# Gathers that leave out the rows of small loads, folds in halves with one job per step, and a store job of its own: a Fourier mixing layer followed by a squared-ReLU feed-forward layer

## The chip, the cores and the metric

The kernel runs on one core of one Trainium2 chip. The metric is the device time of one launch in microseconds (us). Three launches of the kernel before took 628.2, 628.49 and 630.97 us; their median, 628.49 us, is the time before. About 0.5% (3 us) is what a measurement of this kernel can tell from no change.

## The reference, cut to what matters

```
x: (8, 3008, 256) float32      w_in: (256, 2048)      w_out: (2048, 256)
X = fft(fft(x, axis=1), axis=2).real          # per batch of 3008 rows
t = X.reshape(24064, 256)
out = maximum(t @ w_in, 0) ** 2 @ w_out       # float32 (24064, 256)
```

Only the real part is wanted, so the transform along the 3008 rows is a pair of cosine and sine sums, and the transform along the 256 columns can be folded into `w_in`. Rows k and S-k of one batch come from the same two sums with a sign turned, so the kernel computes them together, as a "plus" and a "minus" row.

## The kernel before, in words

**Windows and stages.** The 24064 output rows are computed as 25 windows (`w` = 0 to 24) of up to 512 columns k, each giving a plus and a minus row. Windows 6 to 23 are alike, 512 wide. A window w >= 2 runs eight stages s = 0 to 7; a stage makes 256 of the 2048 hidden features. The order of the instructions on every engine is the order in which the Python code issues them (the schedule is manual); engines wait for each other only through semaphores.

**A plain stage** (`pq`, `turn`): TensorE makes four matmuls of cosines and sines into one PSUM tile `ph` (L808, L809), then 16 matmuls of the second layer of the window before (L679), then two matmuls (L831) that turn the tile into the minus rows. ScalarE applies ReLU to the tile before and after the turn (L840), VectorE squares both (L847).

**A differential stage** (those in `diff[w]`, from window 6 on mostly 0, 2, 4, 6) saves two matmuls: TensorE makes the two cosine matmuls alone (L817); VectorE at once forms `t2` = -2 x cosines + n2 (`twice`, L821); after the 16 matmuls of L679 TensorE adds the sines (L826); ScalarE takes the plus rows out of `ph` (L840) and squares them (L851), VectorE makes the minus rows from `t2` and `ph` in one custom operation (L838). The sines overwrite what `twice` reads, so **L826 waits for L821**, and L821 waits for `n2`, which GpSimd computes with two operations per stage (`nyq_rows`, L769) from a tile `zn` (L760, L761). The rows for window w+1 are issued in the last stages of window w.

**Folds.** The spectrum sums of a batch need its rows added and subtracted in pairs first. Batch number i (0 to 7; the batch index is `bs[i]` = 1 to 7, then 0) is loaded by `load_x` into one buffer `xo` of four quarters (128 partitions x 6 rows of 256 values each, float32 turned into float16 on the way), all from GpSimd's DMA queue: quarters 0 and 1 by a plain DMA (L127), quarters 2 and 3, which must come in reversed row order, by indirect gathers over row indices (L132). Three places need a patch. Row 0 of the batch has to stand in the first place of quarter 2, and for the usual batch VectorE copies it there from quarter 0 (L417; L393 in the first fold). The last batch of `bs` order but one (b = 7, i = 6) has no row after its end to gather, so its index list `idx_c` points the first two partitions to a harmless place, and a small load (L150) overwrites partition 1. Batch 0 (i = 7) has no row before its start, so a gather with the index list `idx_f` fetches quarter 0, and a small load (L143) overwrites one row. The small loads write where a gather has written, and so wait for that gather to land.

**Fold jobs.** `fold_steps(i)` gives the steps: `d_even` (L417 to L419: the copy, then 128x3072 sums into `fe`, then a 128x24 copy), `d_odd` (L422, differences into `fo`), `n_cos` (L429), `n_sin` (L432), `odds` (L435), `even` (L447, and straight after it the store of the folded rows to DRAM, L449), `back` (four loads of these rows in another layout, L457 and L459), `nyq` (two tiny matmuls and a VectorE copy, L440 to L442), and four `late` steps (L473 twice, L484 twice, the last of them followed by the four small copies L490 to L492 of `nyq8`). All sums are VectorE's. For i >= 2 the loop at L728 to L742 places these jobs by hand into the stages: with `b0` = 5, 8, 10, 13, 16, 19 for i = 2 to 7, `d_even` and `n_cos` go to stages 1 and 3 of window b0-1 (5 and 7 for i = 2 and 4), `d_odd` to stage 0 of window b0, `n_sin` and `odds` both to stage 1, `even` and `nyq` to stage 3, `back` to 6, the next `load` to 7, and the late steps to stages 3, 3, 5, 7 of window b0+1. Within a stage these jobs (`others`) are issued after `twice` and the squares of the stage before, and ahead of L838. For i = 0 and 1 the jobs are placed in windows 0 to 4 by the loop over windows (L779 to L796).

Of the kernel before, what the change touches and what calls it, by code (L numbers as in the profile page):

```python
# [12 lines left out]
AF = mybir.ActivationFunctionType  # L13
ALU = mybir.AluOpType

HS = 32.0
P = 128
R = 6


def rev_dim(ap, i):

    dims = [list(d) for d in ap.ap]
    step, cnt = dims[i]
    dims[i] = [-step, cnt]
    return bass.AP(tensor=ap.tensor, offset=ap.offset + step * (cnt - 1), ap=dims)
# [3 lines left out]
def kernel(  # L30
# [51 lines left out]
    def win_of(col):  # L82
        return max(w for w in range(NW) if wins[w][0] <= col) if col < TOT else NW
# [5 lines left out]
    col_of = {}  # L89
# [26 lines left out]
    XW = R * D  # L116

    def load_x(i, first=lambda: None):
        b = bs[i]
        t = xp.tile([P, 4, R, D], F16, name="xo", tag="xo")  # L120
        o = b * S * D

        def flat(q):
            return t[:, q, :, :].rearrange("p c d -> p (c d)")

        def direct(q0, q1):
            nc.gpsimd.dma_start(  # L127
                out=t[:, q0:q1, :, :].rearrange("p q c d -> p q (c d)"),
                in_=bass.AP(tensor=x.tensor, offset=x.offset + o + (q0 * H - 5) * D, ap=[[XW, P], [H * D, q1 - q0], [1, XW]]))

        def gather(q, idx, base):
            nc.gpsimd.indirect_dma_start(  # L132
                out=flat(q), out_offset=None,
                in_=bass.AP(tensor=x.tensor, offset=0, ap=[[XW, B * S * D // XW], [1, XW]]),
                in_offset=bass.IndirectOffsetOnAxis(ap=idx, axis=0),
                element_offset=base)

        if b > 0:
            direct(0, 2)
        else:  # L140

            gather(0, idx["f"][:, 0:1], o + D)
            nc.gpsimd.dma_start(out=t[0:1, 0, R - 1, :], in_=bass.AP(tensor=x.tensor, offset=x.offset + o, ap=[[D, 1], [1, D]]))  # L143
            direct(1, 2)
        first()

        gather(2, idx["r" if b + 1 < B else "c"][:, 0:1], o + (S - R * (P - 1)) * D)
        if b + 1 == B:

            nc.gpsimd.dma_start(  # L150
                out=t[1:2, 2, :, :].rearrange("p c d -> p (c d)"),
                in_=bass.AP(tensor=x.tensor, offset=x.offset + o + (S - R) * D, ap=[[XW, 1], [1, XW]]))
        gather(3, idx["r"][:, 0:1], o + (H - R * (P - 1)) * D)
        return t

    def iota(shape, pattern, base, mult, name):
        t = const.tile(shape, I32, name=name)
        nc.gpsimd.iota(t, pattern=pattern, base=base, channel_multiplier=mult)
        return t

    idx = {}
# [28 lines left out]
    idx["c"] = iota([P, 1], [[1, 1]], P - 1, -1, "idx_c")  # L190
    nc.gpsimd.memset(idx["c"][0:2, :], P - 3)
    idx["f"] = iota([P, 1], [[1, 1]], -1, 1, "idx_f")
    nc.gpsimd.memset(idx["f"][0:1, :], 0)
# [114 lines left out]
    at = const.tile([P, 2, P + 1], F32, name="at")  # L308
# [6 lines left out]
    spn = fop.tile([P, 2, 2, P], F16, name="spn")  # L315
# [53 lines left out]
    def fold_steps(i):  # L369
        t = xs.pop(i)  # L370
# [12 lines left out]
        st = {}  # L383
        xf = t.rearrange("p q c d -> p (q c) d")
        lo = xf[:, :, 1:129]
# [27 lines left out]
                nc.vector.tensor_copy(ev[:, :, 0, 0:1], w[:, :, 0:1])  # L413
            nc.gpsimd.memset(ev[:, :, sg, 129:130], 0.0)

        def d_even():
            nc.vector.tensor_copy(t[0:1, 2, 0, :], t[0:1, 0, R - 1, :])  # L417
            nc.vector.tensor_tensor(fef[:, :, 1:129], lo, hi, op=ALU.add)
# [47 lines left out]
        def fold8(sg):  # L466
            if sg == 0:
                xy = fop.tile([P, 12, 260], F16, name="xy", tag="xy")
                xt = st["xt"] = xy[:, 0:8].rearrange("p (g s r) d -> p g s r d", g=2, s=2)
                yt = st["yt"] = xy[:, 8:12].rearrange("p g (s r d) -> p g s r d", s=1, r=2).rearrange("p (g c) s r d -> p g (c s) r d", g=2)  # L470
                folded[i, 1] = (xt, yt)
            rb = st["rb"]
            nc.vector.tensor_tensor(st["xt"][:, sg], rb[:, 0:2], rev_dim(rb[:, 2:4], 2), op=ALU.subtract if sg else ALU.add)  # L473

        def fold16(sg):

            xt, yt = st["xt"], st["yt"]
# [6 lines left out]
            nc.vector.tensor_tensor(yt[:, sg], both(0), rev_dim(both(1), 2), op=ALU.subtract if sg else ALU.add)  # L484

        def nyq8():

            xt, yt = st["xt"], st["yt"]
            for slot in range(2):
                nc.vector.tensor_copy(xt[:, 0, slot, :, 130:131], rev_dim(xt[:, 1, 1 - slot, :, 128:129], 1))  # L490
# [231 lines left out]
    def put(d, w, s, i, name):  # L722
        d[w][s].append(lambda: folds[i][name]())

    def make(i):
        folds[i] = fold_steps(i)

    for i in range(2, B):  # L728
        b0 = (win_of(col_of[i, 0]) + win_of(col_of[i - 1, 1])) // 2 - 1
        both = i > 2 and len(at_of[b0 - 1][3]) > 0  # L730
        at_of[b0 - 1][0 if i > 2 else 5].append(lambda i=i: make(i))
        put(at_of, b0 - 1, 5 if i == 2 or both else 1, i, "d_even")
        put(at_of, b0 - 1, 7 if i == 2 or both else 3, i, "n_cos")
        for s, name in ((0, "d_odd"), (1, "n_sin"), (1, "odds"), (3, "even"), (6, "back"), (7, "load")):
            put(at_of, b0, s, i, name)
        put(post_of, b0, 3, i, "nyq")
        if b0 > 5:
            diff[b0] = (2, 4, 6)
        for st in range(4):
            at_of[b0 + 1][(3, 3, 5, 7)[st]].append(lambda i=i, st=st: folds[i]["late"][st]())  # L740
        if both:
            diff[b0 - 1] = (2, 6)  # L742
# [29 lines left out]
    for w in range(NW):  # L772
# [231 lines left out]
```

## Time and profile before

| what | value |
|---|---|
| median of three launches | 628.49 us (628.2 to 630.97) |
| the profiled execution | 630.0 us, its span 628.0 us, mean granted TensorE clock 0.994 |
| TensorE (PE) busy | 94% |
| VectorE (DVE) busy | 77% |
| ScalarE (ACT) busy | 73% |
| GpSimd (POOL) busy | 54% |
| moved by DMA | 47.50 MB, mean 76 GB/s |

The span runs from the program's first instruction to its last; some 2 us of the launch lie outside. Busy shares are means over all windows. PE is the engine with the least idle time, so a stall is read best as the idle time in brackets ahead of a PE instruction in the timeline, with the engine and line that ended it. The order of the windows in time follows from the first L808 or L817 of each: for example window 7 starts at 163.56 us, 12 at 290.16, 15 at 365.18, 18 at 443.41, 21 at 522.38.

### The profile page before, as it was taken

To read this page: it belongs to the slowest core of one execution; us is meant where nothing else is said; L and a number is where in the kernel's file an instruction comes from. 1 tells how busy PE (TensorE), PEld (TensorE's weight loads), DVE (VectorE), ACT (ScalarE), POOL (GpSimd) and SP (SyncE) were. 2 spreads that over 40 slices of the span, in tenths; PEclk is the share of its full clock that TensorE was granted. 3 is DMA by queue.
4 is the path that set the end of the run, shared out by engine and by line. 5 is a ranking of instruction groups with operands and counts; after the bars stand their busy time and mean duration, and the time that the engine had idled before them with its cause. 6 is when DMAs were issued, how large, how long until landed. Compare 5 with 4: busy or idle time off the path is not lost.

```text
span 628.0 us, 11263 instructions
## 1 busy us (share of the span) xinstructions
PE 592.7 (94%) x4441; PEld 427.6 (68%) x4441; DVE 484.2 (77%) x607; ACT 460.7 (73%) x624; POOL 338.9 (54%) x248
## 2 busy tenths in 40 slices
PE   4889999999999999999899979999799999999997
PEld 2457786676666776776677746777467776777786
DVE  7787666978888679878887868878588788777760
ACT  6687777878777776877687856878468787787762
POOL 8220225268808617498086673865838558538520
PEclk9999999999999999999999989999899999999999
DMA  8945321124511461236113431132511311111112
GB/s 150 141 89 131 111 69 33 46 81 84 119 41 43 111 137 43 73 78 133 45 36 106 101 74 49 38 108 66 104 33 50 103 47 49 47 39 44 52 55 67
DMA packets 36523, 47.50 MB, mean 76 GB/s; under 512 B 4215, under 2 KB 30327, under 8 KB 36471
## 3 DMA queue, kind: packets, MB, share of 16 engines
q0 software_dynamic: 9344, 22.14, 17.7%
q1 hardware_dynamic: 26899, 24.44, 13.1%
q8 instruction: 34, 0.56, 0.4%
q10 hardware_dynamic: 228, 0.21, 0.1%
q14 instruction: 18, 0.15, 0.1%
HBM read 33.63 MB, written 27.84 MB: 98 GB/s over the span
## 4 chain that ended last, share of the span: by engine, by line
PE 65%; DVE 13%; POOL 9%; DMA 6%; issue 4%; ACT 3%; POOLq 0%; DVEq 0%
PE po L679 37%; PE ph L831 5%; PE ph L808 5%; PE ph L809 5%; POOL n L769 5%; PE ph L826 5%; PE ph L817 3%; PE pz L567 3%; DVE t L821 3%; DVE h L847 3%; DVE h L838 3%; ACT h L840 2%; DMA xo<-in_x_dram,idx_c 2%; DMA xo<-in_x_dram,idx_f 2%; DMA xo<-in_x_dram,idx_r 1%
## 5 line engine op out<-in xcount | busy, mean ns | idle before, releaser
L840 ACT ACTIVATE h<-ph 128x1024 f16<-128x1024 f32 (+3 forms) x311 | 295.6, 990 | 102.2 <-PE ph L826 82.7
L679 PE MATMUL po<-wout,h 128*128 128x256 f16 (+1 forms) x3024 | 362.8, 273 | 0.0
L769 POOL TENSOR_SCALAR n<-zn,g2n 128x512 f32<-128x512 f16 (+2 forms) x146 | 264.8, 1829 | 165.8 <-ACT zn L761 165.5
L679 PEld LDWEIGHTS <-h 128*128 128x128 f16 (+1 forms) x3024 | 297.2, 99 | 73.1 <-issue 1.3
L847 DVE TENSOR_TENSOR h<-h 128x1024 f16<-128x1024 f16 (+6 forms) x216 | 193.8, 908 | 33.4 <-ACT h L840 30.7
L838 DVE CUSTOM_DVE_ANT_0 h<-t,ph 128x1024 f16<-128x1024 f32 x67 | 81.8, 1221 | 47.7 <-ACT h L840 47.3
L821 DVE SCALAR_TENSOR_TENSOR t<-ph,n 128x1024 f32<-128x1024 f32 (+2 forms) x73 | 87.6, 1200 | 29.7 <-PE ph L817 22.3
L808 PE MATMUL ph<-zc,gh 128*128 128x512 f16 (+3 forms) x238 | 88.4, 372 | 0.4 <-ACT h L900 0.3
L809 PE MATMUL ph<-zs,gh 128*128 128x512 f16 (+3 forms) x238 | 88.4, 372 | 0.0
L851 ACT ACTIVATE h<-h 128x1024 f16<-128x1024 f16 (+2 forms) x73 | 76.1, 1043 | 0.0
L831 PE MATMUL ph<-zs,gh 128*128 128x512 f16 (+3 forms) x238 | 68.1, 368 | 0.0
L694 ACT ACTIVATE osb<-po 128x512 f32<-128x512 f32 (+3 forms) x95 | 55.2, 585 | 11.4 <-PE po L679 10.0
L826 PE MATMUL ph<-zs,gh 128*128 128x512 f16 (+2 forms) x146 | 43.6, 380 | 17.0 <-DVE t L821 16.9
L817 PE MATMUL ph<-zc,gh 128*128 128x512 f16 (+2 forms) x146 | 42.8, 375 | 0.0
L809 PEld LDWEIGHTS <-gh 128*128 128x128 f16 x238 | 23.4, 98 | 26.4 <-issue 1.9
L808 PEld LDWEIGHTS <-gh 128*128 128x128 f16 x238 | 23.4, 98 | 25.7 <-issue 1.1
L826 PEld LDWEIGHTS <-gh 128*128 128x128 f16 x146 | 13.8, 97 | 22.6 <-issue 19.4
L572 ACT ACTIVATE es<-pz 128x376 f32<-128x376 f32 (+1 forms) x32 | 15.5, 487 | 17.5 <-PE pz L567 17.4
L831 PEld LDWEIGHTS <-gh 128*128 128x128 f16 x238 | 22.1, 98 | 5.4
L817 PEld LDWEIGHTS <-gh 128*128 128x128 f16 x146 | 14.3, 98 | 16.7
L459 POOL DMA_INDIRECT rb<-scr,idx_r x16 | 20.6, 1288 | 4.9 <-issue 4.9
L132 POOL DMA_INDIRECT xo<-in_x_dram,idx_r x15 | 18.3, 1219 | 4.5 <-issue 4.0
(142 smaller groups left out, 355.3 us busy)
## 6 DMA issues: line engine op xcount, KB each, us to landing
out_dram<-osb SPq DMA_DIRECT2D x77, 128.0 KB
xo<-in_x_dram POOLq DMA_DIRECT2D x7, 768.0 KB
scr<-ev POOLq DMA_DIRECT2D x8, 390.0 KB, 2.8
rb<-scr POOLq DMA_DIRECT2D x16, 130.0 KB
out_dram<-osb SPq DMA_DIRECT2D x12, 94.0 KB
w<-in_moe_w_in_dram POOLq DMA_DIRECT2D x2, 512.0 KB, 11.2
wout<-in_moe_w_out_dram POOLq DMA_DIRECT2D x1, 1024.0 KB
out_dram<-osb SPq DMA_DIRECT2D x8, 75.0 KB
```

The source lines that it names most:

```text
L679: nc.tensor.matmul(po[0:m, j * D : (j + 1) * D], h2[:, fc, q : q + m], wout16[:, fc, :], start=(fc == 0), stop=(fc == NFC - 1))
L769: nc.gpsimd.tensor_scalar(out=n2[:, a, 0:wn1], in0=zns[wt][:, 0:wn1], scalar1=g2n[:, fc : fc + 1], scalar2=None, op0=ALU.mult)
L808: nc.tensor.matmul(ph[:, a, 0:wn], gh[:, 0, f0 : f0 + P], zcw[:, 0:wn], start=True, stop=False)
L809: nc.tensor.matmul(ph[:, a, 0:wn], gh[:, 1, f0 : f0 + P], zsw[:, 0:wn], start=False, stop=True)
L817: nc.tensor.matmul(ph[:, a, 0:wn], gh[:, 0, f0 : f0 + P], zcw[:, 0:wn], start=True, stop=True)
L821: nc.vector.scalar_tensor_tensor(out=t2[:, :, 0:wn], in0=phs[s][:, :, 0:wn], scalar=-2.0, in1=n2s[w, s][:, :, 0:wn], op0=ALU.mult, op1=ALU ...
L826: nc.tensor.matmul(phs[s][:, a, 0:wn], gh[:, 1, f0 : f0 + P], zsw[:, 0:wn], start=False, stop=True, skip_group_check=True)
L831: nc.tensor.matmul(phs[s][:, a, 0:wn], gh[:, 2, f0 : f0 + P], zsw[:, 0:wn], start=False, stop=True, skip_group_check=True)
L838: nc.vector._custom_dve(TENSOR_ADD_SAT, out=h, in0=t2s[s][:, :, 0:wn], in1=phs[s][:, :, 0:wn], s0=BIG, s1=0.0)
L840: nc.scalar.activation(h, phs[s][:, :, 0:wn], AF.Relu, bias=0.0, scale=-1.0)
L847: nc.vector.tensor_tensor(h, h, h, op=ALU.mult)
L851: nc.scalar.activation(h, h, AF.Square, bias=0.0, scale=1.0)
```

## The change

1. **Gathers and small loads apart.** `gather` takes a first partition `p0` and leaves out the partitions ahead of it. For i > 0, quarter 2 is gathered into partitions 1 to 127 only (2 to 127 for b = 7), and a new small load (`rows`: one partition, six rows) fills partition 0 of quarter 2, a second one partition 1 for b = 7. VectorE's copy at the head of `d_even` is dropped. For batch 0 a small load fills partition 0 of quarter 0 first, and the gather takes partitions 1 to 127. The index list `idx_c` goes, `idx_f` becomes a plain count: three small GpSimd instructions fewer at the start. The first load (i = 0) stays as it was.
2. **Halves, one job per step.** `d_even` and `d_odd` can be done in halves (quarters 0 and 1; quarters 2 and 3) for i >= 2, each half in a stage of its own. The 128x24 copy of `d_even` moves to ScalarE and stands ahead of the first half. `n_sin`, `even`, `odds` and the five late steps each get their own stage; `fold16(1)` is parted from `nyq8`, whose four copies become two. In window 9 `diff` becomes (0, 2) in place of (2, 6).
3. **Store.** The store of the folded rows becomes the job `away`, one stage after `even`.

```diff
-        def gather(q, idx, base):
+        def gather(q, idx, base, p0=0):
             nc.gpsimd.indirect_dma_start(
-                out=flat(q), out_offset=None,
+                out=flat(q)[p0:P], out_offset=None,
...
-                in_offset=bass.IndirectOffsetOnAxis(ap=idx, axis=0),
+                in_offset=bass.IndirectOffsetOnAxis(ap=idx[0 : P - p0], axis=0),
                 element_offset=base)
+        def rows(q, p, row, step=D):
+            nc.gpsimd.dma_start(out=t[p : p + 1, q, :, :], in_=bass.AP(tensor=x.tensor, offset=x.offset + o + row * D, ap=[[XW, 1], [step, R], [1, D]]))
...
-            gather(0, idx["f"][:, 0:1], o + D)
-            nc.gpsimd.dma_start(out=t[0:1, 0, R - 1, :], in_=bass.AP(tensor=x.tensor, offset=x.offset + o, ap=[[D, 1], [1, D]]))
+            rows(0, 0, 0, 0)
+            gather(0, idx["f"], o + D, 1)
             direct(1, 2)
...
-        gather(2, idx["r" if b + 1 < B else "c"][:, 0:1], o + (S - R * (P - 1)) * D)
+        p0 = 1 + (b + 1 == B) if i > 0 else 0
+        gather(2, idx["r"], o + (S - R * (P - 1 + p0)) * D, p0)
+        if i > 0:
+            rows(2, 0, 0)
         if b + 1 == B:
-            nc.gpsimd.dma_start(
-                out=t[1:2, 2, :, :].rearrange("p c d -> p (c d)"),
-                in_=bass.AP(tensor=x.tensor, offset=x.offset + o + (S - R) * D, ap=[[XW, 1], [1, XW]]))
-        gather(3, idx["r"][:, 0:1], o + (H - R * (P - 1)) * D)
+            rows(2, 1, S - R)
+        gather(3, idx["r"], o + (H - R * (P - 1)) * D)
...
-        def d_even():
-            nc.vector.tensor_copy(t[0:1, 2, 0, :], t[0:1, 0, R - 1, :])
-            nc.vector.tensor_tensor(fef[:, :, 1:129], lo, hi, op=ALU.add)
-            nc.vector.tensor_copy(fef[:, :, 0:1], xf[:, :, 0:1])
+        def d_even(h=None):
+            a, z = (0, 4 * R) if h is None else (2 * R * h, 2 * R * (h + 1))
+            if a == 0:
+                nc.scalar.activation(fef[:, :, 0:1], xf[:, :, 0:1], AF.Copy, bias=0.0, scale=1.0)
+            nc.vector.tensor_tensor(fef[:, a:z, 1:129], lo[:, a:z], hi[:, a:z], op=ALU.add)
...
-            for slot in range(2):
-                nc.vector.tensor_copy(xt[:, 0, slot, :, 130:131], rev_dim(xt[:, 1, 1 - slot, :, 128:129], 1))
-            nc.vector.tensor_copy(spn[:, 0, :, 0:1], yt[:, 1, 0, :, 128:129])
-            nc.vector.tensor_copy(spn[:, 1, :, 0:1], yt[:, 0, 0, :, 128:129])
+            nc.vector.tensor_copy(xt[:, 0, :, :, 130:131], rev_dim(rev_dim(xt[:, 1, :, :, 128:129], 1), 2))
+            nc.vector.tensor_copy(spn[:, :, :, 0:1], rev_dim(yt[:, :, 0, :, 128:129], 1))
...
     for i in range(2, B):
         b0 = (win_of(col_of[i, 0]) + win_of(col_of[i - 1, 1])) // 2 - 1
+        tight = b0 - 2 in [(win_of(col_of[j, 0]) + win_of(col_of[j - 1, 1])) // 2 - 1 for j in range(2, i)]
+        near = i == 2 or tight
+        at_of[b0 - 1][0].append(lambda i=i: make(i))
+        put(b0 - 1, 5 if near else 1, i, "d_even", 0)
+        put(b0 - 1, (6 if tight else 7) if near else 3, i, "d_even", 1)
+        put(b0 if i == 2 else b0 - 1, 0 if i == 2 else 7 if near else 5, i, "n_cos")
+        put(b0, 0, i, "d_odd", 0)
+        put(b0, 1, i, "d_odd", 1)
+        put(b0, 2, i, "n_sin")
+        put(b0, 3, i, "even")
+        put(b0, 4, i, "away")
+        put(b0, 5, i, "odds")
+        put(b0, 6, i, "back")
+        put(b0, 6, i, "nyq", d=post_of)
+        put(b0, 7, i, "load")
+        for k, s in enumerate((3, 4, 5, 6, 7)):
+            late(b0 + 1, s, i, k)
         if b0 > 5:
             diff[b0] = (2, 4, 6)
+        if tight:
+            diff[b0 - 1] = (0, 2)
```

The lines that the last part replaces are L728 to L742 above. Only i = 4 is `tight` (b0 = 10).

More of the change, by code (lines that the diff above doesn't have):

```diff
@@ L189 @@
     evec_i = iota([P, 2], [[1, 2]], 0, 2, "evec_i")
[L190 to L193, printed above, removed]
+    idx["f"] = iota([P, 1], [[1, 1]], 0, 1, "idx_f")
     def small(shape, name):
@@ L414, in v_part, with d_odd @@
             nc.gpsimd.memset(ev[:, :, sg, 129:130], 0.0)
-        def d_even():
-            nc.vector.tensor_copy(t[0:1, 2, 0, :], t[0:1, 0, R - 1, :])
-            nc.vector.tensor_tensor(fef[:, :, 1:129], lo, hi, op=ALU.add)
-            nc.vector.tensor_copy(fef[:, :, 0:1], xf[:, :, 0:1])
-        def d_odd():
-            nc.vector.tensor_tensor(fof[:, :, 1:129], lo, hi, op=ALU.subtract)
+        def d_even(h=None):
[3 more added lines that the diff above has]
+            nc.vector.tensor_tensor(fef[:, a:z, 1:129], lo[:, a:z], hi[:, a:z], op=ALU.add)
+        def d_odd(h=None):
+            a, z = (0, 4 * R) if h is None else (2 * R * h, 2 * R * (h + 1))
+            nc.vector.tensor_tensor(fof[:, a:z, 1:129], lo[:, a:z], hi[:, a:z], op=ALU.subtract)
         def load():
@@ L447, in even, with away @@
                 nc.vector.tensor_tensor(ev.rearrange("p r c d -> p c r d"), ab[:, :, 0], ab[:, :, 1], op=ALU.add)
+        def away():
             scr = drp.tile([R * P, 260], F16, name="scr", tag="scr")
@@ L488, in nyq8 @@
             xt, yt = st["xt"], st["yt"]
-            for slot in range(2):
-                nc.vector.tensor_copy(xt[:, 0, slot, :, 130:131], rev_dim(xt[:, 1, 1 - slot, :, 128:129], 1))
-            nc.vector.tensor_copy(spn[:, 0, :, 0:1], yt[:, 1, 0, :, 128:129])
-            nc.vector.tensor_copy(spn[:, 1, :, 0:1], yt[:, 0, 0, :, 128:129])
-        late = [lambda: fold8(0), lambda: fold8(1), lambda: fold16(0), lambda: (fold16(1), nyq8())]
-        return {"u_odd": u_odd, "u_part": u_part, "v_even": v_even, "v_part": v_part, "d_even": d_even, "n_cos": n_cos, "odds": odds, "d_odd": d_odd, "load": load, "n_sin": n_sin, "nyq": nyq, "even": even, "back": back, "late": late}
+            nc.vector.tensor_copy(xt[:, 0, :, :, 130:131], rev_dim(rev_dim(xt[:, 1, :, :, 128:129], 1), 2))
+            nc.vector.tensor_copy(spn[:, :, :, 0:1], rev_dim(yt[:, :, 0, :, 128:129], 1))
+        late = [lambda: fold8(0), lambda: fold8(1), lambda: fold16(0), lambda: fold16(1), nyq8]
+        return {"u_odd": u_odd, "u_part": u_part, "v_even": v_even, "v_part": v_part, "d_even": d_even, "n_cos": n_cos, "odds": odds, "d_odd": d_odd, "load": load, "n_sin": n_sin, "nyq": nyq, "even": even, "away": away, "back": back, "late": late}
     gh = const.tile([P, 3, F], F16, name="gh")
@@ L714, in fold_jobs @@
         f = folds[i] = fold_steps(i)
-        return [f["d_even"], f["n_cos"], lambda: (f["d_odd"](), f["load"]()), f["n_sin"], f["odds"], f["nyq"], f["even"], f["back"]]
+        return [f["d_even"], f["n_cos"], lambda: (f["d_odd"](), f["load"]()), f["n_sin"], f["odds"], f["nyq"], lambda: (f["even"](), f["away"]()), f["back"]]
     NST = NFC // 2
@@ L720, with put, late @@
     diff = {w: (0, 2, 4, 6) if w > 5 else (4, 6) for w in range(4, NW)}
-    def put(d, w, s, i, name):
-        d[w][s].append(lambda: folds[i][name]())
+    def put(w, s, i, name, *k, d=at_of):
+        d[w][s].append(lambda: folds[i][name](*k))
+    def late(w, s, i, *st):
+        at_of[w][s].append(lambda: run(*[folds[i]["late"][k] for k in st]))
     def make(i):
@@ L729 @@
         b0 = (win_of(col_of[i, 0]) + win_of(col_of[i - 1, 1])) // 2 - 1
[L730 to L736, printed above, removed]
+        tight = b0 - 2 in [(win_of(col_of[j, 0]) + win_of(col_of[j - 1, 1])) // 2 - 1 for j in range(2, i)]
[15 more added lines that the diff above has]
+            late(b0 + 1, s, i, k)
         if b0 > 5:
             diff[b0] = (2, 4, 6)
[L739 to L742, printed above, removed]
+        if tight:
+            diff[b0 - 1] = (0, 2)
     n2s = {}
@@ L784 @@
             te = table_steps(1)
-            at = [[folds[1]["even"]], [lambda: te["freq"](), lambda: te["args"](0)], [lambda: f0s["v_part"](0)], [lambda: f0s["v_part"](1), f0s["even"], f0s["back"]],
+            at = [[folds[1]["even"], folds[1]["away"]], [lambda: te["freq"](), lambda: te["args"](0)], [lambda: f0s["v_part"](0)], [lambda: f0s["v_part"](1), f0s["even"], f0s["away"], f0s["back"]],
                   [lambda: te["turns"](0)], [lambda: te["mods"](0)], [lambda: te["absm"](0), lambda: te["sins"](0)], [lambda: te["coss"](0)]]
@@ L788 @@
             at[0] = [lambda: te["weigh"]()]
-            for st in range(4):
-                at[1 + st // 2] = at[1 + st // 2] + f0s["late"][st : st + 1]
+            for st in range(5):
+                at[1 + st // 3] = at[1 + st // 3] + f0s["late"][st : st + 1]
             at[3] = [folds[1]["back"]]
@@ L793 @@
         elif w == win_of(col_of[1, 1]) - 1:
-            for st in range(4):
-                at[st] += folds[1]["late"][st : st + 1]
+            for st in range(5):
+                at[min(st, 3)] += folds[1]["late"][st : st + 1]
             lo, hi = 4, NST - 1
```

## The prediction

> **What bounds the kernel.** The page's first part:
>
> ```profile
> PE 592.7 (94%) x4441; PEld 427.6 (68%) x4441; DVE 484.2 (77%) x607; ACT 460.7 (73%) x624; POOL 338.9 (54%) x248
> ```
>
> TensorE is idle 35 of 628 us, so what can go fast is that idle time, and what the clock loses. Its waits, longest first (total, times, longest in us):
>
> ```profile
> PE ph L826 <- DVE t L821: 16.9, 13, 4.5
> ```
>
> This line is all of PE's idle time behind 50 us (the other waits are of the first 50). L826 adds the sines in a differential stage and needs L821, on VectorE. The timeline gives the thirteen: 1.07 us at 114; 0.53 at 166 and 1.47 at 174; 0.55 at 198; 0.34 at 236; 0.64 at 249; 0.64 at 293 and 1.85 at 300; 3.79 at 371 and 0.33 at 379; 4.47 at 450 and 0.57 at 458; 0.64 at 525. They have three causes. The first, at 371 (start, length, engine, instruction, idle time before it):
>
> ```profile
> 364.94 0.57 POOL L150 DMA_DIRECT2D xo<-in_x_dram  x1 [9.64 <-DMA xo<-in_x_dram,idx_c]
> 365.18 0.59 PE L817 MATMUL ph<-zc,gh 128*128 128x512 f16 x2
> ...
> 366.86 14.69 POOL L769 TENSOR_SCALAR n<-zn,g2n 128x512 f32<-128x512 f16 x8
> ...
> 370.04 1.23 DVE L821 SCALAR_TENSOR_TENSOR t<-ph,n 128x1024 f32<-128x1024 f32 x1 [2.99 <-POOL n L769]
> ...
> 371.32 1.01 PE L826 MATMUL ph<-zs,gh 128*128 128x512 f16 x2 [3.79 <-DVE t L821]
> ...
> 372.55 0.63 PE L809 MATMUL ph<-zs,gh 128*128 128x512 f16 x1
> ```
>
> GpSimd's small load (L150) waited 9.64 us for the gather before it to land. Behind it, in GpSimd's order, stand the last gather and the n2 rows; L821 got its rows at 370.04 in place of 365.8, and PE stood 3.79 us. At 441 us it is the same for batch 0: L143 waited 8.92 us for its gather, and PE stood 4.47 us. What follows is a lower clock (window, length, busy us of PE, PEld, DVE, ACT, POOL, then the granted clock):
>
> ```profile
> 365.18:394.08 28.90, 24.78 (x171) 16.96 (x169) 21.81 (x28) 17.58 (x22) 17.47 (x11) 0.94 0.22 51
> 443.41:473.05 29.64, 24.59 (x171) 16.91 (x170) 21.44 (x28) 17.49 (x22) 18.21 (x11) 0.94 0.35 73
> 522.38:546.00 23.62, 22.98 (x170) 16.53 (x169) 18.34 (x23) 17.63 (x23) 13.38 (x9) 1.00 0.15 43
> 371.15:374.57 3.42, 3.25 (x10) 1.38 (x10) 2.05 (x3) 1.52 (x2) 3.42 (x3) 0.50 0.00 0
> 449.66:453.08 3.42, 2.85 (x8) 1.13 (x8) 2.10 (x3) 1.12 (x2) 3.42 (x3) 0.50 0.55 112
> ```
>
> Windows 15 and 18 (the first two rows) took 28.90 and 29.64 us, window 21, which has no fold, 23.62. In the 3.42 us behind each stall the clock was 0.50; matmuls of 0.38 us took 0.63.
>
> The other two causes stand in window 12, at 293 and 300:
>
> ```profile
> 290.16 0.59 PE L817 MATMUL ph<-zc,gh 128*128 128x512 f16 x2
> ...
> 290.84 0.42 DVE L484 TENSOR_TENSOR xy<-xy 128x520 f16<-128x520 f16 x1
> 291.18 0.65 DVE L490 COPY xy<-xy 128x2 f16<-128x2 f16 x2
> ...
> 291.88 1.21 DVE L821 SCALAR_TENSOR_TENSOR t<-ph,n 128x1024 f32<-128x1024 f32 x1
> ...
> 293.14 0.59 PE L826 MATMUL ph<-zs,gh 128*128 128x512 f16 x2 [0.64 <-DVE t L821]
> ...
> 296.61 0.59 PE L817 MATMUL ph<-zc,gh 128*128 128x512 f16 x2
> 296.83 0.48 DVE L417 COPY xo<-xo 1x256 f16<-1x256 f16 x1
> ...
> 297.35 2.19 DVE L418 TENSOR_TENSOR fe<-xo 128x3072 f16<-128x3072 f16 x1
> ...
> 299.55 1.21 DVE L821 SCALAR_TENSOR_TENSOR t<-ph,n 128x1024 f32<-128x1024 f32 x1
> ...
> 300.81 0.59 PE L826 MATMUL ph<-zs,gh 128*128 128x512 f16 x2 [1.85 <-DVE t L821]
> ```
>
> At 290.84 VectorE still does the last late step and four small copies (0.42 + 0.65 + 0.32, overlapping; 1.04 us from first start to 291.88), so L821 starts at 291.88, while its cosines began at 290.16. Where nothing precedes it, L821 starts 0.6 us behind the cosines. At 296.83 it is the copy of one row, the 2.19 us sum and the copy of 24 columns: L821 starts 2.94 us behind its cosines.
>
> **The change, part by part.** PE has 0.43 us of cosines and 1.75 us of second-layer matmuls before the sines; L821 takes 1.2 us from start to sines. It may thus start 1.0 us behind the cosines before PE stalls.
>
> *Gathers apart.* The order of the changed kernel's instructions shows no wait of a small load for the gather ahead of it; the waits left are for DMAs eight issues earlier. In window 14 GpSimd then issues, from 353.19: plain load, gather, two small loads, gather: 0.79 + 1.01 + 2 x 0.57 + 0.99 us and four pauses of 0.3, so 358.0. The signal for the rows of window 15 comes 20 us after a window's start (285.42 against 265.43 in window 11), so at 360.4: no wait left, 2.4 us spare. In window 17: small load, gather, plain, gather, small load, gather from 431.6, some 0.57 + 1.1 + 0.6 + 1.0 + 0.57 + 1.0 and five pauses of 0.3: 438.0, the signal at 438.7. Both stalls go: 3.79 + 4.47 = 8.26 us. The clock with them: PE's 3.25 and 2.85 busy us at half clock would take half, 3.05 us. Each other load gains one small load, 0.57 + 0.3 us on GpSimd. In windows 5, 8, 10 that lies in GpSimd's idle time (2.31 us before the rows at 158.64, 15.80 before 238.69, 3.10 before 285.42). For i = 1 it doesn't: the last gather is issued at 27.36 and VectorE waits 1.5 us for it at 35.75, on the way to PE's 1.90 us stall at 46.91. Between 0 (the DMA engines are busy anyway) and 0.87 us; I take 0.4. Three start-up instructions less bring L214, 0.4 us early (11.20 for 11.60), on the way to the first cosine table; I take 0.2 gained.
>
> *The nyq8 copies.* With the last sum one stage earlier and two copies for four, VectorE has some 0.4 us where it had 1.04: L821 starts 0.7 us earlier. The stalls 0.53, 0.64 and 0.64 go, 1.8 us, and the same ones under the stalls at 371 and 450 don't come to light.
>
> *The halves.* Half of 2.19 (or of 1.79, which it takes with GpSimd quiet) and 0.06 us of start is 0.95 to 1.15 us. The row copy and the 24-column copy are gone from VectorE. L821 at 299.55 comes at about 296.61 + 0.22 + 1.1 = 297.95, 1.3 us behind its cosines: 0.3 us of 1.85 is left. The second half meets stage 4 as `n_cos` (0.96 us) does now, where PE doesn't wait. Gone are 1.07, 1.2 of 1.47, 0.34 (window 9's differential stages now lie ahead of the fold), 1.55 of 1.85 and 0.33 and 0.57: 5.0 us. Windows 15 and 18, so far shielded, get 0.3 each: 4.4.
>
> *One job per step.* `n_sin` and `odds` (0.96 + 1.2 us) leave stage 1, where they made L821 late at 198 and 249: 0.55 + 0.64 = 1.2 us. They land in stages 2 and 5: `n_sin` behind L821 where VectorE now idles 0.6 to 0.8 us before L838, `odds` with 1.2 us where `n_cos` fits with 0.96; 0.05 us in each of five windows, 0.2 us lost.
>
> *ScalarE's copy* (0.2 us by L419) waits for the whole load. For i = 4 that may hurt: in window 8 the rows for window 9 now come ahead of the load, four (`back`'s DMAs excepted) in place of two, 3.4 us, and the small load 0.9: the last gather goes from 218.4 to 223 and lands by the median of 10.2 us at 233; the copy stands at 230.5. Behind it on ScalarE are the ReLUs that free `ph`. ScalarE is 73% busy and catches up 0.7 us in a stage, PE has one tile to spare: 0 to 2.5 us, I take 0.4.
>
> *The store* is issued when `even` ends, as before; it only stands later in the program. Nothing.
>
> Sum: 8.26 + 3.05 + 1.8 + 4.4 + 1.2 + 0.2 - 0.4 - 0.2 - 0.4 = 17.9. Whole stages, from their first matmul to the next stage's in the timeline, give 0.7 us more: the two stalls with the slow stage behind them are 6.94 + 4.25 and 7.62 + 4.05 us against 2.61 + 3.04 undisturbed, 11.6 in place of 11.3, and the late stages of window 12's kind lose 0.80, not 0.64. So 18.6 us: the profiled execution's 630.0 (span 628.0 and 2.0 around it) becomes **611**. It lies 1.5 us above the median of the three launches, which would come to 610.
>
> **Rivals.** *(1) Only the two big stalls go.* VectorE is 22 of 25.7 us busy in window 12, and jobs that are spread may only spread the lateness. For it: each half costs nearly what `n_cos` does, and there are more of them. Against: the delay before L821 counts, not the sum. Then 11.3 us are gained: 618.7, 616 to 622.
>
> *(2) Slower: a gather of 127 rows runs on few DMA engines.* All gathers of the trace have 128 rows:
>
> ```profile
> q0 software_dynamic: 9344, 22.14, 17.7%
> ...
> xo<-in_x_dram,idx_r POOLq DMA_INDIRECT x15, 10.2
> ```
>
> Of 16 engines, 17.7% of 628 us for 22.14 MB are 80 us per MB on one engine. A gather of 127 rows (0.39 MB) takes 2 us spread on 16 and 31 us on one; it would land 29 us later. Batches 1, 3, 4, 5 are needed 0, 7, 6 and 8 us after they land now (the sums at 35.75, 170.84, 233.41, 297.35 against issue plus 10.2), batch 7 some 7 (issue 432.5 against 450): 29 + 22 + 23 + 21 + 22 = 117 us, and ScalarE's copy stops PE with it: 611 + 117 = 728. It decides from about 9.5 us of extra landing, where 9.5 + 2.5 + 3.5 + 1.5 + 2.5 eat the gain, that is with two engines or fewer (13.5 later; three 8.4). For it: the stores of 128 rows at 241 us take the DMA engines to 50 to 90% busy for a little over 1 us, those of 71, 57, 37 and 91 rows at 254 us to 10 to 20% for 3 us, so on SP's queue the row count decides. Against: GpSimd's queue makes its own packets, here one per partition with an index each, and shows no such case.
>
> The Trainium skill (DMA: Bandwidth & Descriptors, "Why a DMA increments its semaphore by 16 and not by 1") says that a DMA uses the largest number of engines, up to 16, that divides its row count, 127 rows one, with an exception for some plain copies of GpSimd; SP's stores here agree, gathers aren't named as excepted. By it the kernel would be slower, as in (2).
>
> *(3) The wait stays* (the gather's end is waited for elsewhere, by ScalarE's copy): stages as before, 628 to 631. The order of instructions speaks against it.
>
> **How the numbers follow.** Forecast (605 to 616) 0.65; (1) 0.16; (2) 0.16; (3) 0.03. The range takes in forecast and (1), 605 to 622: its ends hold the bounds of ScalarE's wait (2.1 more), the first load (0.5), the halves (0.95 to 1.15 and none lost: 1.5 less) and the 1.5 us between launches. Faster by over 0.5% (3 us): 0.65 + 0.16 = 0.81; within: 0.03; slower: 0.16.
>
> **What would show it.** Right: the two waits of GpSimd's small loads (9.6, 8.9) gone; PE's wait for L821 down from 16.9 to 1 to 3 us; no clock of 0.50 in mid-span; windows 7, 12, 15, 18 at 23 to 24.5 us. Wrong: long waits of ScalarE or VectorE for x's gathers, in window 1 first (rival 2); PE's wait still over 5 us in short pieces (rival 1).

## The result, and the profile after

Four launches of the changed kernel took 762.70 to 764.02 us, median **763.47 us**, beside 629.73 us (628.2 to 631.89) of the kernel before: 1.212 times as long (95% interval 1.2075 to 1.2165). The profiled execution took 764.02 us, its span 762.2 us. The forecast was 611, the range 605 to 622; what came is rival (2), for which the prediction had worked out 728.

The page of the changed kernel: engines (busy us, share, instructions), the granted TensorE clock in 40 slices, and GpSimd's DMA queue (packets, MB, share of 16 engines):

```profile
PE 604.8 (79%) x4441; PEld 432.3 (57%) x4441; DVE 480.7 (63%) x589; ACT 462.5 (61%) x631; POOL 350.6 (46%) x252
...
PEclk9966986999995999669995899999995899999999
...
q0 software_dynamic: 22912, 22.19, 15.8%
```

TensorE's busy share falls from 94% to 79%, and the clock drops in six places. GpSimd's queue moves the same 22 MB (22.19 for 22.14) in 22912 packets in place of 9344. TensorE's longest waits (total, times, longest in us), and those for x's gathers and for the store of the folded rows:

```profile
PE ph L845 <- ACT h L854: 72.4, 3, 27.3
PE ph L822 <- ACT h L854: 46.1, 3, 22.1
PE ph L840 <- DVE t L835: 23.0, 10, 20.4
```

```profile
ACT fe L420 <- DMA xo<-in_x_dram,idx_r: 98.9, 4, 28.4
...
POOL ev L415 <- DMA scr<-ev: 28.6, 1, 28.6
DVE fe L421 <- DMA xo<-in_x_dram,idx_r: 28.6, 1, 28.6
```

(Lines have moved: L822 and L823 are the plain stage's cosines and sines, L831 and L840 the differential ones, L835 is `twice`, L854 the ReLU, L420 ScalarE's copy of 24 columns, L421 the even half sum, L845 the turn, L415 GpSimd's small clears in `ev`, L132 the gather, L139 the small load.) In before TensorE waited 16.9 us for `twice` and never for ScalarE behind 50 us. The names alone would put the blame on the ReLU; the second list tells that ScalarE itself stood 98.9 us, at the copy that waits for the gathers. One of the six stalls, in the timeline (start, length, engine, instruction, idle time before it and what ended it):

```profile
201.74 2.61 POOL L132 DMA_INDIRECT xo<-in_x_dram,idx_r  x1 [0.30 <-issue]
...
241.39 0.31 ACT L420 ACTIVATE fe<-xo 128x24 f16<-128x24 f16 x1 [23.03 <-DMA xo<-in_x_dram,idx_r]
...
242.47 1.03 ACT L854 ACTIVATE h<-ph 128x1024 f16<-128x1024 f32 x1
...
243.55 0.58 PE L822 MATMUL ph<-zc,gh 128*128 128x512 f16 x1 [22.08 <-ACT h L854]
```

The gather of 127 rows for i = 3, issued at 201.74, landed 37.8 us later, and the one of 128 rows behind it, issued at 205.25, 36.1 us later; until then ScalarE stood at its copy, 23.03 us, the ReLUs behind it freed no `ph`, and TensorE stood 22.08 us. What the DMA engines did meanwhile, beside the same gather with 128 rows in the experiment `mixed` below (window, length, busy us of PE, PEld, DVE, ACT, POOL, granted clock, mean busy share of the 16 DMA engines, GB/s):

```profile
218.00:239.00 21.00, 3.47 (x30) 2.42 (x28) 2.82 (x3) 0.36 (x1) 3.11 (x2) 0.70 0.07 14
...
566.00:584.00 18.00, 1.48 (x14) 1.17 (x12) 0.00 (x0) 0.00 (x0) 3.04 (x2) 0.64 0.14 30
```

```profile
154.00:162.00 8.00, 7.72 (x54) 5.05 (x52) 7.70 (x13) 6.80 (x10) 5.15 (x4) 1.00 0.99 199
```

A share of 0.07 is one engine of sixteen (1/16 = 0.063), at 14 GB/s; with 128 rows and the plain load the share is 0.99 at 199 GB/s. At 566 us two gathers of 127 rows are under way (batch 0 has two), on two engines: 0.14 and 30 GB/s.

The stalls of TensorE over 2 us, behind 50 us, beside rival (2)'s figures:

| fold i | stall at | measured us | rival (2) |
|---|---|---|---|
| 1 | 64.09 | 25.64 | 29 |
| 2 | 121.50 | 19.51 | nothing |
| 3 | 243.55 | 22.08 | 22 |
| 4 | 333.62 | 27.26 | 23 |
| 5 | 420.11 | 21.78 | 21 |
| 7 | 587.93, 591.15 | 20.45 + 2.20 | 22 |

i = 6 (b = 7), whose gather has 126 rows, shows none.

### The profile page after: what moved, and what is told of

It is laid out like the page before. It is cut to its first block, busy times and chain, and to the rows that moved or that the text cites. A ratio compares the mean times of both kernels' runs of the same rounds, so it can differ in the third digit from the quotient of the medians.

```text
span 762.2 us, 11278 instructions
## 1 busy us (share of the span) xinstructions
PE 604.8 (79%) x4441; PEld 432.3 (57%) x4441; DVE 480.7 (63%) x589; ACT 462.5 (61%) x631; POOL 350.6 (46%) x252
## 3 DMA queue, kind: packets, MB, share of 16 engines
q0 software_dynamic: 22912, 22.19, 15.8%
## 4 chain that ended last, share of the span: by engine, by line
PE 49%; DMA 27%; POOL 12%; DVE 6%; issue 4%; ACT 3%; ACTq 0%; POOLq 0%; DVEq 0%
PE po L682 28%; DMA xo<-in_x_dram,idx_r 23%; POOL n L783 6%; PE ph L822 4%; PE ph L823 4%; PE ph L845 4%; DMA scr<-ev 4%; PE ph L840 3%; PE ph L831 2%; POOL xo L132 2%; PE pz L570 2%; DVE h L861 2%; ACT h L854 1%; POOL rb L464 1%; DVE h L852 1%
## 5 line engine op out<-in xcount | busy, mean ns | idle before, releaser
L783 POOL TENSOR_SCALAR n<-zn,g2n 128x512 f32<-128x512 f16 (+2 forms) x146 | 262.0, 1809 | 261.4 <-ACT zn L775 261.1
L682 PE MATMUL po<-wout,h 128*128 128x256 f16 (+1 forms) x3024 | 369.6, 276 | 0.0
L854 ACT ACTIVATE h<-ph 128x1024 f16<-128x1024 f32 (+3 forms) x311 | 295.8, 990 | 88.1 <-PE ph L840 63.3
L682 PEld LDWEIGHTS <-h 128*128 128x128 f16 (+1 forms) x3024 | 300.6, 100 | 77.6 <-issue 3.8
L861 DVE TENSOR_TENSOR h<-h 128x1024 f16<-128x1024 f16 (+6 forms) x216 | 197.6, 925 | 86.4 <-ACT h L854 83.8
L845 PE MATMUL ph<-zs,gh 128*128 128x512 f16 (+3 forms) x238 | 70.1, 377 | 72.4 <-ACT h L854 72.4
L822 PE MATMUL ph<-zc,gh 128*128 128x512 f16 (+3 forms) x238 | 90.4, 380 | 46.4 <-ACT h L854 46.1
L835 DVE SCALAR_TENSOR_TENSOR t<-ph,n 128x1024 f32<-128x1024 f32 (+2 forms) x73 | 87.6, 1200 | 22.7 <-PE ph L831 21.9
L823 PE MATMUL ph<-zs,gh 128*128 128x512 f16 (+3 forms) x238 | 90.3, 380 | 0.0
L420 ACT ACTIVATE fe<-xo 128x24 f16<-128x24 f16 x7 | 2.2, 308 | 125.1 <-DMA xo<-in_x_dram,idx_r 98.9
L865 ACT ACTIVATE h<-h 128x1024 f16<-128x1024 f16 (+2 forms) x73 | 76.1, 1043 | 0.0
L845 PEld LDWEIGHTS <-gh 128*128 128x128 f16 x238 | 22.5, 99 | 78.8 <-issue 73.0
L823 PEld LDWEIGHTS <-gh 128*128 128x128 f16 x238 | 23.8, 100 | 73.8 <-issue 50.1
L840 PE MATMUL ph<-zs,gh 128*128 128x512 f16 (+2 forms) x146 | 43.2, 377 | 23.0 <-DVE t L835 23.0
L421 DVE TENSOR_TENSOR fe<-xo 128x1536 f16<-128x1536 f16 (+1 forms) x13 | 13.4, 1029 | 48.7 <-DMA xo<-in_x_dram,idx_r 28.6
L831 PE MATMUL ph<-zc,gh 128*128 128x512 f16 (+2 forms) x146 | 42.8, 375 | 0.0
L822 PEld LDWEIGHTS <-gh 128*128 128x128 f16 x238 | 23.8, 100 | 26.7 <-issue 2.8
L132 POOL DMA_INDIRECT xo<-in_x_dram,idx_r x16 | 27.0, 1690 | 4.8 <-issue 4.6
L840 PEld LDWEIGHTS <-gh 128*128 128x128 f16 x146 | 13.3, 97 | 27.7 <-issue 24.7
L127 POOL DMA_DIRECT2D xo<-in_x_dram x8 | 6.4, 796 | 46.8 <-DVE fo L425 38.7
```

What stands on the lines that cost most here:

```text
L682: nc.tensor.matmul(po[0:m, j * D : (j + 1) * D], h2[:, fc, q : q + m], wout16[:, fc, :], start=(fc == 0), stop=(fc == NFC - 1))
L783: nc.gpsimd.tensor_scalar(out=n2[:, a, 0:wn1], in0=zns[wt][:, 0:wn1], scalar1=g2n[:, fc : fc + 1], scalar2=None, op0=ALU.mult)
L822: nc.tensor.matmul(ph[:, a, 0:wn], gh[:, 0, f0 : f0 + P], zcw[:, 0:wn], start=True, stop=False)
L823: nc.tensor.matmul(ph[:, a, 0:wn], gh[:, 1, f0 : f0 + P], zsw[:, 0:wn], start=False, stop=True)
L831: nc.tensor.matmul(ph[:, a, 0:wn], gh[:, 0, f0 : f0 + P], zcw[:, 0:wn], start=True, stop=True)
L835: nc.vector.scalar_tensor_tensor(out=t2[:, :, 0:wn], in0=phs[s][:, :, 0:wn], scalar=-2.0, in1=n2s[w, s][:, :, 0:wn], op0=ALU.mult, op1=ALU ...
```

## The experiments

The theory: a gather of 127 rows runs on one DMA engine; all the rest of the change does what the forecast says, some 613 us. Rivals: the small loads or the longer issue on GpSimd cost the time; only gathers that are needed at once cost it; not the divisor counts but an odd row count, or the first partition; the new order of the folds has a part in the loss. All ratios are to the kernel before on the same chip.

### g126: the same loads with gathers of 126 rows

```diff
-            gather(0, idx["f"], o + D, 1)
+            rows(0, 1, 1)
+            gather(0, idx["f"], o + (R + 1) * D, 2)
...
-        p0 = 1 + (b + 1 == B) if i > 0 else 0
+        p0 = 2 if i > 0 else 0
...
-        if b + 1 == B:
-
             rows(2, 1, S - R)
```

From i = 1 on, each gather that had 127 rows leaves out two partitions, and two small loads fill them: one row less on the gather, one DMA more.

> Changed: every gather of the changed kernel that has 127 rows gets 126 instead, and one more small load per place fills the row that is left out. Theory A (a gather is spread on the largest number of DMA engines up to 16 that divides its row count: 127 on 1, 126 on 14): the gathers land in about 10 us as the one of 126 rows in the changed kernel does (9.57), all stalls of 20 to 27 us go, and the time is what the forecast gave, 611, plus up to 2 us for seven more small loads of 0.9 us on GpSimd: 609 to 615 us. Theory B (the loss is ScalarE's copy standing in front of the ReLUs and waiting for x, whatever the gather takes): the copy still waits in windows 1, 7, 9, 12, 18, and the time stays above 680 us. Theory C (a gather that does not begin at partition 0, or a small load beside it, is slow): as now, about 763 us.

Measured: 612.94 us (611.45 to 616.58), ratio 0.9705 (0.9646 to 0.9765). The gathers of 126 rows land 8.5 to 11.6 us behind their issue, where the 127-row ones took 34.9 to 39.0. All x gathers together (count, median us to landing), and TensorE's longest wait behind 50 us (for `twice`):

```profile
xo<-in_x_dram,idx_r POOLq DMA_INDIRECT x16, 8.8
```

```profile
PE ph L839 <- DVE t L834: 2.7, 10, 0.3
```

No stall of TensorE over 0.4 us is left behind 50 us. One row fewer takes 150 us off. The small loads are not the cost, there being more of them here.

### mixed: 128 rows, VectorE's copy of the one row, the new order

Relative to the changed kernel:

```diff
-            gather(0, idx["f"], o + D, 1)
+            nc.gpsimd.dma_start(out=flat(0)[1:P], in_=bass.AP(tensor=x.tensor, offset=x.offset + o + D, ap=[[XW, P - 1], [1, XW]]))
...
-        p0 = 1 + (b + 1 == B) if i > 0 else 0
+        p0 = 2 if b + 1 == B else 1 if i in () else 0
...
+                if h and bs[i] + 1 < B and i not in ():
+                    nc.vector.tensor_copy(t[0:1, 2, 0, :], t[0:1, 0, R - 1, :])
+                nc.scalar.activation(fef[:, a:z, 0:1], xf[:, a:z, 0:1], AF.Copy, bias=0.0, scale=1.0)
```

(`i in ()` is never true; the next experiment puts a number there.) The copy of row 0 stands ahead of the second half, ScalarE's copy is in halves too, and quarter 0 of batch 0 comes by a plain DMA of 127 rows.

> Changed: quarter 2 is gathered with all 128 rows again and VectorE copies the one row, as in the kernel before, except for the batch with no row after its end (126 rows and two small loads); batch 0's quarter 0 comes by a plain DMA of 127 rows beside its small load in place of a gather of 127; ScalarE's column copy is cut in halves with the sums. Nothing then waits on GpSimd for a gather. Theory A: 608 to 613 us, the forecast less the extra small loads. If a plain DMA of 127 rows goes on one engine as well, window 18 stalls for about 20 us: 630 to 636. Theory B or C: ScalarE's copy still waits, above 620 us.

Measured: 613.05 us (612.83 to 615.85), ratio 0.9714 (0.9664 to 0.9764); span 611.4, clock 1.00. The plain DMA of 127 rows among the DMA issues (KB each, us to landing):

```profile
xo<-in_x_dram POOLq DMA_DIRECT2D x1, 381.0 KB, 7.8
```

It lands in 7.8 us: the row count alone doesn't decide, the kind of DMA does too. TensorE's waits behind 50 us (L845 is the sines, L840 `twice`, L850 the turn, L859 the ReLU):

```profile
PE ph L845 <- DVE t L840: 2.7, 10, 0.3
...
PE ph L850 <- ACT h L859: 1.1, 1, 1.1
```

### only2: one gather of 127 rows, for a fold that has time

`mixed`, but i = 2 alone with the changed kernel's load:

```diff
-        p0 = 2 if b + 1 == B else 1 if i in () else 0
+        p0 = 2 if b + 1 == B else 1 if i in (2,) else 0
```

VectorE's copy of the one row goes for i = 2, since the small load brings it. Batch 2 isn't needed before window 4; the prediction's rival (2) names no cost for it.

> Changed against the mixed kernel: the gather of batch i = 2 alone has 127 rows (and a small load). Batch 2 is first needed near 110 us, long after it could land even with 35 us. Theory A with a queue: the folded rows of batches 1 and 0, stored and read back near 57 to 72 us, have shares on the one busy DMA engine behind the 127 rows and come late; PE stalls about 20 us at the end of window 2 and the clock halves: 18 to 27 us over the mixed kernel. Rival (my prediction's working): only who needs the gathered rows waits, so batch 2 costs nothing: within 1 us of the mixed kernel.

Measured: 633.19 us (632.48 to 635.31), ratio 1.003 (1.0006 to 1.0054), 20 us over `mixed`, in one stall of 19.24 us at 94.18. Packets of GpSimd's queue rise from 9392 to 11328. The wait that explains it (GpSimd, for a store to land):

```profile
POOL ev L414 <- DMA scr<-ev: 28.3, 1, 28.3
```

It is not batch 2 that is late but the store of folded rows issued behind its gather: it landed 28.9 us after its issue, where it takes 2.8 in `mixed`. In the changed kernel the same store took 29.2 us where the median is 4.3, and there the chain runs on:

```profile
113.05 0.57 DVE L368 TENSOR_TENSOR ev<-w 128x768 f16<-128x768 f16 x1 [24.10 <-DMA scr<-ev]
...
119.24 0.83 ACT L275 ACTIVATE sin<-m 128x754 f16<-128x754 f32 x1 [20.59 <-DVE m L269]
119.98 1.47 ACT L854 ACTIVATE h<-ph 128x752 f16<-128x752 f32 x2
...
121.50 0.78 PE L845 MATMUL ph<-zs,gh 128*128 128x376 f16 x2 [19.51 <-ACT h L854]
```

The store holds the buffer `ev` that VectorE writes next; VectorE, waiting there, is late with `m`, which ScalarE's sines need; and the ReLU stands behind the sines. So a transfer on one engine delays a DMA that the queue issues behind it.

### sizes: six row counts

`mixed`, but quarter 2 of i = 2 to 7 is gathered with 125, 122, 113, 112, 126 and 120 rows; a second gather and small loads fill the rest.

```diff
+        p0 = 2 if b + 1 == B else {2: 3, 3: 6, 4: 15, 5: 16, 7: 8}.get(i, 0)
...
+        if p0 > 2:
+            nc.gpsimd.indirect_dma_start(
+                out=flat(2)[1:p0], out_offset=None,
```

> Changed against the mixed kernel: quarter 2 of batches i = 2, 3, 4, 5, 6, 7 is gathered with 125, 122, 113, 112, 126, 120 rows, and a second gather of 2, 5, 14, 15, 0, 7 rows and small loads fill the rest. Theory A (largest divisor up to 16): engines 5, 2, 1, 16, 14, 15, so rows on one engine 25, 61, 113, 7, 9, 8; at 0.25 us a row and 3 to 6 us around it the gathers land 10 to 13, 18 to 22, 31 to 35, 8 to 11, 9 to 11, 8 to 11 us after issue. Rival (an odd row count goes on one engine, an even one on many): 34 to 38, 10, 31 to 35, 10, 10, 10 us. Rival (any gather short of 128 that begins at an odd partition is slow): 125, 113 slow, the others 10 us. The packets of GpSimd's queue tell too: 127 rows brought 15 x 127 packets of 4 bytes more.

Measured: 636.56 us in one launch, span 634.8. Landing of the six gathers from their issue:

| rows | largest divisor up to 16 | expected us | landed us | issue on GpSimd us |
|---|---|---|---|---|
| 125 | 5 | 10 to 13 | 11.38 | 1.53 |
| 122 | 2 | 18 to 22 | 21.56 | 1.73 |
| 113 | 1 | 31 to 35 | 32.59 | 2.43 |
| 112 | 16 | 8 to 11 | 11.44 | 0.98 |
| 126 | 14 | 9 to 11 | 9.86 | 1.05 |
| 120 | 15 | 8 to 11 | 11.67 | 1.89 |

125 is odd and fast, 122 even and slow, 112 starts at partition 16 and 113 at 15: neither oddness nor the place decides, the divisor does. The rows of 112 and 120 landed a little above their range, about where 128 rows land at the same places in `mixed` (10.75 and 10.94 us). The trace's packets give the engines a second time (last section). This is the rule of the Trainium skill (DMA: Bandwidth & Descriptors, "Why a DMA increments its semaphore by 16 and not by 1") that the prediction cited; the runs agree for gathers, and agree with its exception for the plain copy of 127 rows. Only the one-engine gather stalls TensorE for long (L856 is the turn, L865 the ReLU):

```profile
258.49 1.01 PE L856 MATMUL ph<-zs,gh 128*128 128x512 f16 x2 [19.46 <-ACT h L865]
```

The two-engine one (i = 3) cost 0.70 us at 180.36. Its gather landed 13.1 us later than that of 128 rows in `mixed` (21.56 against 8.43). In this kernel ScalarE's copy is in halves, so its first half waits for no gather; for i = 3 the changed kernel's waits for the whole load two stages earlier.

### loads_only: the change's loads in the old order

The kernel before with the changed `load_x`, the row copy dropped; whole sums, all copies on VectorE, no job moved.

> The loads of the change (gathers of 127 rows, 126 for b = 7, and the small loads) under the schedule, the whole sums and the copies of the kernel before. Theory (the loss is the gathers' alone; the new order of the folds neither makes it nor softens it): PE's long stalls come back with six of 20 to 27 us, some 139 us in all, on VectorE's whole sum in place of ScalarE's column copy, and the time is that of the changed kernel plus the 5.9 us that the new order was worth by itself: 769 us, 760 to 778. Rival (ScalarE's copy, which the new order puts ahead of the ReLUs and which waits for the whole load, makes a good part of the loss): with that copy back on VectorE the stalls are shorter by some microseconds each, and the time is 720 to 750 us.

Measured: 772.11 us (770.24 to 772.24), ratio 1.2225 (1.2185 to 1.2266). Six stalls of 17.58 to 27.55 us (145.5 in all); five come now by VectorE's whole sum, and the one of i = 2 (17.58) by the late store as before:

```profile
DVE fe L418 <- DMA xo<-in_x_dram,idx_r: 127.1, 5, 29.5
...
PE ph L826 <- DVE t L821: 105.9, 13, 25.6
```

ScalarE's copy was only the place where the wait showed. On balance the new order makes none of the loss: without it the ratio is 1.2225 in place of 1.212, their intervals apart.

### sched_only and mixed_old: one half each

`sched_only` is the new order with the loads of before; `mixed_old` is the order of before with `mixed`'s loads (no small load waits for a gather there, all gathers have 128 or 126 rows). The main lines of the first's edit:

```diff
-        p0 = 1 + (b + 1 == B) if i > 0 else 0
-        gather(2, idx["r"], o + (S - R * (P - 1 + p0)) * D, p0)
+        gather(2, idx["r" if b + 1 < B else "c"][:, 0:1], o + (S - R * (P - 1)) * D)
```

> The changed kernel's schedule (halves, one job per step, store apart, ScalarE's column copy, now cut in halves) with the loads of the kernel before: 128-row gathers, small loads that wait for them, the row copy on VectorE. The mixed kernel took 613.1. If the terms of the prediction add, the two stalls behind GpSimd's waits come back, 3.79 + 4.47 us and 3.05 us of clock: 613 + 11 = 624 us, 621 to 627. Rival (the two stalls cover the schedule's gain in windows 15 and 18, and little else was gained): 627 to 631, no change.

> The mixed kernel's loads (nothing on GpSimd waits for a gather, no gather of 127 rows) with the schedule of the kernel before. By the prediction's terms windows 15 and 18 fall from 28.9 and 29.6 us to what window 12 takes (25.7), since the lateness of VectorE that the stalls covered comes to light: 630.5 - 7.1 = 623, 621 to 626. Rival (the whole gain of the mixed kernel is the two waits): 613 to 616.

Measured: `sched_only` 624.88 us (623.25 to 625.77), ratio 0.9907 (0.9878 to 0.9936); `mixed_old` 621.81 (621.29 to 623.43), ratio 0.986 (0.983 to 0.9891). TensorE's wait for `twice`, first `sched_only`, then `mixed_old`:

```profile
PE ph L844 <- DVE t L839: 9.9, 8, 4.5
```

```profile
PE ph L826 <- DVE t L821: 11.8, 13, 1.9
```

The first keeps the two big stalls (3.77 and 4.47 us), the second all the small ones. Alone they gain 5.9 and 8.9 us, together (`mixed`) 17.5. The missing 2.7 us is no more than the intervals of the three runs allow, but TensorE's stalls go the same way: in `mixed_old` the whole sums of i = 6 and 7, no longer shielded by the big stalls, stall TensorE 0.92 and 1.86 us, where they cost 0.33 and 0.57 before.

### mixed_whole and mixed_late: single parts of the new order

`mixed` with the big sums whole; `mixed` with four late copies as in the kernel before, issued together with the last sum:

```diff
-        put(b0 - 1, 5 if near else 1, i, "d_even", 0)
-        put(b0 - 1, (6 if tight else 7) if near else 3, i, "d_even", 1)
+        put(b0 - 1, 5 if near else 1, i, "d_even")
...
-        put(b0, 0, i, "d_odd", 0)
-        put(b0, 1, i, "d_odd", 1)
+        put(b0, 0, i, "d_odd")
```

```diff
-        for k, s in enumerate((3, 4, 5, 6, 7)):
+        for k, s in enumerate((3, 4, 5, 7, 7)):
```

> The mixed kernel with the two big sums whole again, each in the stage of its first half. By the prediction's term for the halves 4.4 us come back, in windows 4, 7, 12, 15 and 18: 613 + 4.4 = 617.5 us, 616 to 619. Rival (halves only spread the same work on a busy VectorE): within 1 us of 613.

> The mixed kernel with the last sum and four small copies together again in the last stage, as before. By the term for these copies, 0.6 to 0.8 us come back at the start of each of windows 7, 12, 15, 18 and 21: 613 + 3.5 = 616.5 us, 615.5 to 617.5. Rival (they are hidden once the folds are halved): 613 to 614.

Measured: `mixed_whole` 620.64 us (620.33 to 622.65), ratio 0.9837 (0.9812 to 0.9861): 7.6 us over `mixed`, more than expected. TensorE's wait for `twice` there:

```profile
PE ph L843 <- DVE t L838: 9.4, 11, 2.0
```

That is 6.7 us more than `mixed`'s 2.7: stalls of 1.59, 1.97, 1.03 and 1.97 us at 176, 301, 375 and 449, of which the halves leave nothing at the first and 0.21 or 0.22 at the others (the prediction left 0.3), and one of 0.98 at 116; and the clock fell to 0.50 for 3.4 us at 450, behind the 1.97, and at 48. `mixed_late` 616.3 us (613.85 to 617.2), ratio 0.9762 (0.9733 to 0.9792), which overlaps `mixed`'s interval: by the times this stays inconclusive. TensorE's wait rises from 2.7 to 3.6 us; the five late stages stall 0.52 to 0.64 us in place of 0.32.

## Why the prediction was wrong, point by point

**The failed step** is in "Gathers apart": it gave a gather of 127 rows the landing and the issue of one of 128 (10.2 and 1.0 us), and then in the choice between forecast and rival (2) at 0.65 against 0.16. The runs showed 34.9 to 39.0 us and 2.6 to 2.9 us. For the forecast the prediction had only that GpSimd's queue makes its own packets, one per partition. That says how many packets there are, not which engine gets them. No row showed a gather of another count, while the DMA engines' low share under SP's stores of 71, 57, 37 and 91 rows, and the cited rule, both pointed to few engines. The two cases lay 117 us apart, and the unmeasured one should have ruled the range at least.

**Rival (2)'s sum.** Its five stalls came to 117 us; the same five measure 119.4. It was short in two terms. Batch 2 was left out, and cost 19.5 by what queues behind it (`only2`). And the clock was left out: TensorE's busy time is 604.8 us against 589.8 in `mixed`, 15.0 us lost at a clock of 0.50 in six stretches of 20.5 to 27.3 us from within each stall. Against `mixed`, idle time of TensorE is 152.8 for 17.0 us: 135.8 + 15.0 = 150.8, the whole difference of the spans (762.2 - 611.4).

**It decides from two engines or fewer:** not in `sizes`, where two engines cost 0.70 us. That kernel's ScalarE copy waits later, so for the changed kernel the point stays open.

**The other steps, in kernels whose gathers spread.** There the forecast's 611 became 612.94 (`g126`) and 613.05 (`mixed`), within its own 605 to 616; the gain of the profiled span was 16.0 and 16.6 us against 18.6. The mechanisms held, but several sizes were off and in part made up for each other, so that the sum lies so near is luck to that extent:

- *Gathers apart* (8.26 + 3.05): both waits of small loads gone, TensorE's busy time 592.7 to 589.8 in `mixed` by the clock, 2.9 for 3.05. Right.
- *Nyq8 copies* (1.8): far too large. Of the 0.53 to 0.64 us, 0.32 is left, and that in five windows, since it comes to light in windows 15 and 18 too, where the big stalls hid it before: 1.81 us of stalls became 5 x 0.32 = 1.60. In `mixed` the two copies still hold `twice` from 287.42 to 287.98, 0.56 us where the prediction has 0.4.
- *Halves* (4.4): a little too small. In `g126` the six stalls of the whole sums, 5.63 us, became three of 0.22, 4.97 us less; beside whole sums that no big stall shields (`mixed_whole`) it is 6.7. The stall before the fold of i = 2 (1.07) goes in `g126`; in `mixed` ScalarE's copy waits there 1.11 us for VectorE's copy of the one row, and TensorE stands 1.12.
- *One job per step* (1.2 - 0.2): the stalls at 198 and 249 (0.55 + 0.64) are gone, and two of 0.28 and 0.22 us are new, where a late sum and `even` now stand ahead of `twice` (160.09 and 202.39 in `mixed`). No run has this part alone.
- *First load* (-0.4): too small where small loads stand ahead of the last gather. Window 1 took 23.96 us in `g126` (two small loads there), 21.62 in `mixed` (none) and 21.81 before.
- *ScalarE's copy* (-0.4): nothing seen in `g126`, where it waits for the whole load as well: no stall over 0.4 us.
- *Store, start-up*: no stall is due to the store's job. Window 1 begins at 31.75 before and 31.77 in the changed kernel: of the 0.2 us at the start nothing is seen.

## What to carry to other kernels

Before a gather's row count is changed, look at how many engines the new count uses, and keep a count with a large divisor up to 16: overwrite one row afterwards, or leave out one more, rather than gather 127. A shape that the trace doesn't show is no small variation of one that it does. And a transfer on one engine is paid for not only by its reader but by the DMAs that its queue issues while it runs; one that isn't needed yet can stop the kernel through another's buffer.

## What the runs showed of the hardware that was not expected

- **Each 127-row gather adds 1905 packets of 4 bytes, 15 x 127.** `only2` has 1936 packets more on GpSimd's queue than `mixed`, for one gather of 127 rows and one small load. By the trace's sizes 1921 of them have 4 bytes and 16 have 192, and one of 3072 is missing. Every DMA of this queue brings 16 packets of 4 bytes (70 DMAs and 1120 such packets in the kernel before), and a small load 16 of 192; that leaves 1905. So each of the 15 engines without data gets as many packets as the one with data, though hardly more bytes (22.19 MB for 22.14). For the ten gathers that `sizes` changes or adds, the same reckoning with their divisors gives 2869 packets of 4 bytes, and 160 for the ten DMAs more; the trace has 3029 more than `mixed`, which is their sum.
- **GpSimd is held longer too**, the longer the fewer engines are used: issuing a gather of 127 rows took 2.6 to 2.9 us in place of 1.0. In `sizes`, beside the gather of 128 rows at the same place in `mixed`, it took 2.43 us for 1.01 at one engine, 1.73 for 1.02 at two and 1.53 for 1.28 at five; at fifteen (1.89 for 1.87) and sixteen (0.98 for 1.01) there is no difference. Less than 2 us a gather is no match for stalls of 20; these end when the gathers land.
- **The clock** was granted in stretches whose lengths are multiples of some 3.41 us. In the changed kernel it fell to 0.50 within each long stall and came back 3.35 to 5.93 us after the end of one (the stall ending at 243.55, the clock back at 246.90); only behind the stall at 587.93, with 2.20 us more to follow, it took 7.12. A stall of 1.97 us in `mixed_whole` brought it down at 449 but not at 301, and the grid of 3.41 us tells why: the first lies within one interval, the second is cut by a border at 300.24. Over all eleven traces, from the first full clock to the last matmuls, TensorE was idle for 1.97 us or more in each of the 21 intervals behind which the clock fell, and for 1.98 us at most in those behind which it stayed full.
